# Four batches of memory attention in front of two feed-forward layers: keys, values and softmax laid out anew for batches 1 to 3

## The chip, the cores and the metric

One core of one Trainium2 chip. The time is device microseconds of one execution; lower is better. Engines in the rows: PE is TensorE (PEld its weight loads), DVE VectorE, ACT ScalarE, POOL GpSimd, SP the engine that issues all transfers here. DMA stands for the 16 transfer engines.

## The reference

There are 4 batches, 8 heads, 576 tokens, 64 values per head and 32 memory slots. Both feed-forward layers are 512 to 2048 to 512 over 4 x 576 = 2304 tokens.

```python
a = exp(phi - max(phi, tokens)); a = a / (sum(a, tokens) + 1e-9)
k_m = einsum('bhsm,bhsd->bhmd', a, k); v_m = einsum('bhsm,bhsd->bhmd', a, v)
scores = q @ k_m.T / 8                    # 576 x 32 per head
attn = softmax(scores)                    # over the 32 slots, 1e-9 added to the sum
x = attn @ v_m                            # heads side by side: 2304 x 512
h = x @ w_in;  x = max(0.01 * h, h) @ w_out
h = x @ w_in2; out = (h * tanh(log(1 + exp(h)))) @ w_out2
```

## The kernel before

The first layer runs over chunks of 288 tokens. Its hidden blocks come from the attention weights and from `v_m` multiplied into `w_in` (`win_t` by `vT_t`, line 793, giving `vw_t`). Line 1044 makes a hidden block `h_t` from `at_t` and `vw_t`; line 1077 accumulates the output `acc_t`. Operands are split into a high part (`hi_t`, rounded) and a low part (`lo_t`, the rest), and products of high and low parts are summed. The second layer works on 768 tokens at a time with seven products instead of eight (lines 1398 and 1551), and its results leave at lines 1586 to 1600 as blocks of 128 rows by 256 columns, from `x_t` and `ob_t`, into `out`.

The attention of batches 1 to 3 is done in between, for each of two groups of four heads:

- `kv_tasks`: loads `phi`, `k`, `v` with 96 rows that hold six tokens each. VectorE folds the maxima over the six (line 521), TensorE transposes them (535), VectorE reduces and makes a diagonal matrix (541, 549), TensorE spreads it over the rows (555), VectorE subtracts (562), ScalarE takes exp, VectorE folds the sums (521), TensorE sums over the rows (590) and makes the key and value memories (579, 24 small matmuls per group). `kv_norm` scales them and TensorE transposes the result (626).
- `score_tasks`: loads the queries; TensorE transposes them, three blocks at a time (673), VectorE or ScalarE copies them out. `scores` makes the scores (707) for both halves of 288 tokens. `half` does the softmax on VectorE and ScalarE, in 32 x 32 blocks that VectorE transposes (727 to 757), and splits the weights into `at_t`.

The order is not written down. Each step is a task with a price per engine and a due time, and the class `Order` simulates the engines with these prices: whenever one is free it takes the ready task that is due first, and the instructions are issued in that order. A buffer that several steps share (`Tag`, `Ring`) is handed on when its last user has ended in this simulation. A table `K` holds the due times: batch 1's attention is due 10 units before its first use (`A1`), the later ones 30 (`A2`); loads of the second layer's operands (`tscr` into `wo_t`) are due 5 units ahead (`L4T`). All transfers go through SP in one queue.

Of the kernel before, what the change touches and what calls it, by code (L numbers as in the profile page):

```python
# [10 lines left out]
F32R = mybir.dt.float32r  # L11
# [12 lines left out]
def hop(a, b):  # L24
# [10 lines left out]
    DW=280e3, DQ=1.3, DP=1.2, DS=0.78, DI=0.38, L4=0.5, L4P=1.6, L4S=0.8, L4T=5.0, MA=6, FK=-52.5, DWF=0.85, MV="......rvvrrvvrvr",  # L35
# [124 lines left out]
def kernel(  # L160
# [266 lines left out]
    def kv_first(g, p0, dp):  # L427
        sp = "s" if g else ""
        ph = tags["phi" + sp].new([P, 576] if sp else [P, HG * R * M])
        kv = tags["kv" + sp].new([P, 2304] if sp else [P, 2 * HG * R * D])  # L430
# [70 lines left out]
    def kv_tasks(b, g, p0, dp):  # L501
        if not b:
            return kv_norm(b, g, p0, dp, *kv_first(g, p0, dp))
        sp, ps_tag = "", misc
        ph = tags["phi" + sp].new([PR, HG, R, M])
        kv = tags["kv" + sp].new([P, 2, HG, R, D])
        hs = slice(g * HG, (g + 1) * HG)
        pl = p0 - 6
        l_phi = load(pl, ph.make, lambda: phi[b, hs].rearrange("h (p r) m -> p h r m", p=PR), 294912, (), [ph], (), K["DP"])

        def ld(e):
            kv.make()
            for j, x in enumerate((k, v)):
                dma(out=kv.t[:PR, j], in_=x[b, hs].rearrange("h (p r) d -> p h r d", p=PR))

        l_kv = add({"SP": K["DQ"] * mb(1179648)}, pl + 0.2, ld, (), [kv])

        def fold(buf, op):

            halves = [ph.t[:, :, r:r + R // 2].rearrange("p h r m -> p r h m") for r in (0, R // 2)]  # L520
            nc.vector.tensor_tensor(out=buf.make(), in0=halves[0], in1=halves[1], op=op)
            for r in range(NR, R // 2):
                nc.vector.tensor_tensor(out=buf.t[:, 0], in0=buf.t[:, 0], in1=buf.t[:, r], op=op)


        NR = R // 2 if b < 2 else 1

        rmax = tags["rm" + sp].new([PR, R // 2, HG, M])
        t0 = keep(add({"DVE": 0.58 if b < 2 else 1.1}, p0, lambda e: fold(rmax, ALU.max), [l_phi], [rmax], [ph]))
        mt = ps_tag.new([P, NR, PR])  # L530

        def fmt(e):
            mt.make()
            for r in range(NR):
                nc.tensor.transpose(mt.t[:, r], rmax.t[:, r].rearrange("p h m -> p (h m)"), ident[:PR, :PR])

        t1 = add({"PE": 0.1 + 0.1 * NR}, p0 + dp, fmt, [t0], [mt], [rmax])
        mx, dg = tags["mx" + sp].new([P, 1]), tags["dg" + sp].new([P, P])
        t2 = add(
            {"DVE": dve(NR * PR)}, p0 + dp,  # L540
            lambda e: nc.vector.tensor_reduce(out=mx.make(), in_=mt.t.rearrange("p r c -> p (r c)"), axis=AX.X, op=ALU.max),
            [t1], [mx], [mt],
        )

        def fdg(e):
            if e == "ACT":
                nc.scalar.activation(out=dg.make(), in_=ident, func=AF.Copy, scale=mx.t)
            else:
                nc.vector.tensor_scalar(out=dg.make(), in0=ident, scalar1=mx.t, scalar2=None, op0=ALU.mult)

        t2 = add({"ACT": 0.21, "DVE": 0.21}, p0 + dp, fdg, [t2], [dg], [mx])
        bc = ps_tag.new([PR, HG, 1, M])
        t3 = add(
            {"PE": 0.25}, p0 + 2 * dp,
            lambda e: nc.tensor.matmul(
                out=bc.make().rearrange("p h o m -> p (h o m)"), lhsT=ones, rhs=dg.t, start=True, stop=True
            ),
            [t2], [bc], [dg, mx],
        )
        t4 = add(  # L560
            {"DVE": 0.87}, p0 + 2 * dp,
            lambda e: nc.vector.tensor_tensor(
                out=ph.t, in0=ph.t, in1=bc.t.to_broadcast([PR, HG, R, M]), op=ALU.subtract
            ),
            [t3], (), [ph, bc],
        )
        t5 = [add(
            {"ACT": act(768)}, p0 + 2.5 * dp,
            lambda e: nc.scalar.activation(out=ph.t, in_=ph.t, func=AF.Exp), [t4], (), [ph],
        )]  # L570
        rs = tags["rm" + sp].new([PR, R // 2, HG, M])
        t6 = add({"DVE": 0.58 if b < 2 else 1.1}, p0 + 3 * dp, lambda e: fold(rs, ALU.add), t5, [rs], [ph])
        acc, dn = ps_tag.new([P, 2 * D]), misc.new([P, 1])

        def fkv(e):
            acc.make()
            for r in range(R):
                for h in range(HG):
                    nc.tensor.matmul(  # L579
                        out=acc.t[M * h:M * (h + 1), :].rearrange("p (j d) -> p j d", j=2),  # L580
                        lhsT=ph.t[:, h, r, :],
                        rhs=kv.t[:PR, :, h, r, :],
                        start=(r == 0),
                        stop=(r == R - 1),
                    )

        def fsums(e):
            dn.make()
            for r in range(NR):
                nc.tensor.matmul(  # L590
                    out=dn.t, lhsT=rs.t[:, r].rearrange("p h m -> p (h m)"), rhs=ones[:PR, 0:1],
                    start=(r == 0), stop=(r == NR - 1),
                )

        den, rec = tags["den" + sp].new([P, 1]), tags["rec" + sp].new([P, 1])

        t6 = add(
            {"PE": 0.2 * NR}, p0 + 3.5 * dp, fsums, [t6], [dn], [rs],
        )
        t7 = add({"PE": 1.65}, p0 + 3.8 * dp, fkv, [*t5, l_kv, t6], [acc], [ph, kv])  # L600
# [5 lines left out]
        t8 = add({"DVE": 0.25}, p0 + 4.0 * dp, fden, [t6], [den, rec], [dn])  # L606

        kv_norm(b, g, p0, dp, acc, rec, t7, t8)

    def kv_norm(b, g, p0, dp, acc, rec, t7, t8):  # L610
        sp = "s" if b < K['SB'] and g == 1 else ""
        kvn = tags["kvn" + sp].new([P, 2 * D])
# [8 lines left out]
        kt = (misc if b else acc_tag.slots[1]).new([P, P])  # L621
        kb, vb = kT_tag[g].new([P, P]), vT_tag.new([P, HG // 2, M])

        def ftr(e):
            kt.make(), kb.make(), vb.make()
            nc.tensor.transpose(kt.t, kvn.t, ident)

        t11 = add({"PE": 0.12}, p0 + 5 * dp, ftr, [t9], [kt, kb, vb], [kvn])

        ks, vs = [], []  # L630
        for j in range(2):
# [7 lines left out]
                lambda e, x=half_j, j=j: copy(e, vb.t[x], kt.t[D:2 * D].rearrange("p (a e m) -> p e a m", e=2, m=M)[:, j]),  # L639
# [5 lines left out]
    def score_tasks(b, g, pq, ps, dp):  # L645
        sp = b < K['SB'] and g == 1
        qT = (qT_s if sp else qT_tag).new([P, HG, NB1])
        parts, firsts_q = [], []
        qb = (q_s if sp else q_tag).new([P, RQ, D])
        q_g = q[b, g * HG:(g + 1) * HG]  # L650

        def ld(e):
            qb.make()
            if not b:
                dma(out=qb.t, in_=q_g.rearrange("h (p r) d -> (h p) r d", r=RQ))
                return
            for h in range(HG):
                dma(
                    out=qb.t[32 * h:32 * (h + 1)].rearrange("p (j r) d -> p j (r d)", r=2),
                    in_=q_g[h].rearrange("(j p r) d -> p j (r d)", r=2, p=32),  # L660
                )

        lq = add({"SP": (K["DQ"] if b else K["DS"]) * mb(589824)}, pq - 4 if b else PQ[g], ld, (), [qb])
        for i in range(3):
            ps_b = (misc if b else h_tag).new([P, 3, P])

            def ftr(e, ps_b=ps_b, i=i):
                ps_b.make()
                if not i:
                    qT.make()  # L670
                for j in range(3):
                    r = 2 * (3 * i + j)
                    nc.tensor.transpose(ps_b.t[:, j], qb.t[:, r:r + 2, :].rearrange("p r d -> p (r d)"), ident)  # L673

            tt = add({"PE": 0.34}, pq + 0.7 * i, ftr, [lq, *firsts_q[:1]], [ps_b] if i else [ps_b, qT], [qb])
# [15 lines left out]
        both = scores(b, g, ps[0], qT, parts, (0, 1)) if b else None
# [967 lines left out]
```

## Time and profile before

| | |
|---|---|
| median of 3 runs | 750.68 us (750.11 to 751.19) |
| the profiled execution | 751.77 us, of which its span is 750.0 |
| granted TensorE clock, mean | 0.997 of full |
| TensorE busy | 737.4 us, 98% |
| VectorE busy | 545.8 us, 73% |
| ScalarE busy | 413.1 us, 55% |
| transfers | 183.75 MB, 245 GB/s on the mean |

The span runs from the first to the last record of the core; the time of a run has some more around it. A busy share says how much of the span an engine had an instruction running, not how close to its peak. The chain goes back from the last instruction, each time to what released it; its shares say who the others waited for.

### The profile page before, as it was taken

How to read it: one execution, taken by the hardware profiler on the slowest of the kernel's cores; microseconds unless marked ns; L12 is line 12 of the kernel's file. 1: busy time of each engine (PE TensorE's matmuls, PEld its weight loads, DVE VectorE, ACT ScalarE, POOL GpSimd, SP SyncE). 2: the span in 40 equal slices, each digit the busy share in tenths (PEclk: the TensorE clock that was granted, in tenths of full speed). 3: DMA queues.
4: the chain of work that ended last, by engine and by line, in shares of the span. 5: the costliest groups of instructions: out<-in, count | busy, mean ns of one | idle time of the engine just before them, and what ended most of it. 6: DMA issues, size and time to landing. Idle time of an engine off the chain costs nothing.

```text
span 750.0 us, 15892 instructions
## 1 busy us (share of the span) xinstructions
PE 737.4 (98%) x5978; PEld 706.4 (94%) x5978; DVE 545.8 (73%) x1180; ACT 413.1 (55%) x916; POOL 0.7 (0%) x6
## 2 busy tenths in 40 slices
PE   8899999999999999999999999999999999999997
PEld 7689899988898998999999999999999999999997
DVE  6989758768676886655779798767576965665585
ACT  3867457646464656554456674644455644454443
POOL 0000000000000000000000000000000000000000
PEclk9999999999999999999999999999999999999999
DMA  9984595838869397966269988788977878987476
GB/s 345 294 286 136 176 285 169 245 122 263 239 222 320 141 300 241 308 193 215 99 247 317 351 321 293 226 265 258 322 250 245 266 246 254 290 289 224 126 214 193
DMA packets 99436, 183.75 MB, mean 245 GB/s; under 512 B 8224, under 2 KB 55328, under 8 KB 99360
## 3 DMA queue, kind: packets, MB, share of 16 engines
q1 hardware_dynamic: 99360, 182.75, 75.8%
q8 instruction: 47, 0.77, 0.4%
q14 instruction: 29, 0.24, 0.1%
HBM read 140.25 MB, written 42.47 MB: 244 GB/s over the span
## 4 chain that ended last, share of the span: by engine, by line
PE 90%; DVE 3%; DMA 3%; ACT 2%; issue 1%; SPq 0%; ACTq 0%; DVEq 0%
PE acc_t L1077 25%; PE h_t L1398 21%; PE acc_t L1551 17%; PE h_t L1044 12%; PE misc_t L1551 7%; PE misc_t L793 2%; PE acc_t L1398 2%; DMA q_t<-in_q_dram 1%; PE acc_t L485 1%; PE misc_t L579 1%; DMA rawm_t<-in_moe_w_in_dram 1%; DMA raw_t<-w2scr 1%; PE misc_t L673 1%; PE misc_t L707 1%; DVE vw_t L326 0%
## 5 line engine op out<-in xcount | busy, mean ns | idle before, releaser
L1077 PE MATMUL acc_t<-hi_t,wo_t 128*128 128x288 f32 x1024 | 163.3, 299 | 0.9 <-ACT x_t L310 0.8
L1077 PEld LDWEIGHTS acc_t<-hi_t,wo_t 128*128 128x128 f32 x1024 | 143.2, 188 | 14.0 <-issue 9.3
L1551 PE MATMUL acc_t<-wo_t,hi_t 128*128 128x256 f32 x720 | 133.7, 279 | 0.0
L1044 PE MATMUL h_t<-at_t,vw_t 128*128 128x288 f32 x768 | 124.7, 298 | 2.7 <-ACT e_t L1058 0.9
L1551 PEld LDWEIGHTS acc_t<-wo_t,hi_t 128*128 128x128 f32 x720 | 118.0, 188 | 0.2 <-DVE ob_t L312 0.2
L1044 PEld LDWEIGHTS h_t<-at_t,vw_t 128*128 128x128 f32 x768 | 109.8, 189 | 4.0 <-ACT e_t L1058 1.4
L1058 ACT ACTIVATE hi_t<-h_t 128x288 fp32r<-128x288 f32 x128 | 52.4, 410 | 110.6 <-PE acc_t L1077 89.4
L1551 PE MATMUL acc_t<-wo_t,lo_t 128*128 128x256 f32 x360 | 102.0, 283 | 0.0
L1065 DVE TENSOR_TENSOR lo_t<-e_t,hi_t 128x288 fp32r<-128x288 f32 x128 | 57.7, 454 | 54.7 <-ACT e_t L1058 28.5
L1077 PE MATMUL acc_t<-lo_t,wo_t 128*128 128x288 f32 x512 | 91.2, 300 | 0.2 <-DVE lo_t L1065 0.2
L1398 PE MATMUL h_t<-xt_t,vw_t 128*128 128x384 f32 x396 | 79.2, 336 | 0.0
L1077 PEld LDWEIGHTS acc_t<-lo_t,wo_t 128*128 128x128 f32 x512 | 74.7, 188 | 4.5 <-issue 3.6
L1520 DVE TENSOR_TENSOR lo_t<-wo_t,hi_t 128x384 fp32r<-128x384 f32 x94 | 52.0, 555 | 36.9 <-ACT hi_t L310 35.5
L1398 PE MATMUL h_t<-xt_t,wo_t 128*128 128x384 f32 x352 | 75.5, 336 | 0.0
L1551 PEld LDWEIGHTS acc_t<-wo_t,lo_t 128*128 128x128 f32 x360 | 67.6, 188 | 0.0
L1398 PEld LDWEIGHTS h_t<-xt_t,vw_t 128*128 128x128 f32 x396 | 66.7, 188 | 0.5 <-DVE wo_t L1417 0.5
L310 ACT ACTIVATE hi_t<-wo_t 128x384 fp32r<-128x384 f32 x83 | 43.4, 523 | 41.0 <-PE acc_t L1551 28.4
L1398 PEld LDWEIGHTS h_t<-xt_t,wo_t 128*128 128x128 f32 x352 | 59.5, 188 | 0.1
L1551 PE MATMUL misc_t<-wo_t,hi_t 128*128 128x256 f32 x288 | 54.1, 279 | 0.0
L1058 ACT ACTIVATE e_t<-h_t 128x288 f32<-128x288 f32 x128 | 51.8, 407 | 0.0
L1520 DVE TENSOR_TENSOR lo_t<-vw_t,hi_t 128x384 fp32r<-128x384 f32 x50 | 27.7, 555 | 25.4 <-ACT hi_t L310 25.2
L1423 ACT ACTIVATE wo_t<-wo_t 128x384 f32<-128x384 f32 x53 | 27.6, 521 | 32.9 <-DVE wo_t L1417 32.7
(219 smaller groups left out, 1079.0 us busy)
## 6 DMA issues: line engine op xcount, KB each, us to landing
wo_t<-tscr SPq DMA_DIRECT2D x168, 256.0 KB, 3.9
vw_t<-wsum SPq DMA_DIRECT2D x32, 512.0 KB, 4.7
win_t<-wscr SPq DMA_DIRECT2D x24, 512.0 KB, 5.9
raw_t<-in_moe_w_in_dram SPq DMA_DIRECT2D x19, 512.0 KB, 6.9
raw_t<-in_moe_w_out_dram SPq DMA_DIRECT2D x17, 512.0 KB, 7.7
wsum<-vw_t SPq DMA_DIRECT2D x16, 512.0 KB, 5.1
wo_t<-wsum SPq DMA_DIRECT2D x16, 512.0 KB, 4.3
kv_t<-in_k_dram SPq DMA_DIRECT2D x8, 576.0 KB, 9.8
```

The costliest lines, as they stand in the source:

```text
L310: nc.scalar.activation(out=o, in_=i, func=AF.Copy)
L485: nc.tensor.matmul(out=acc.t[rows, :].rearrange("p (j d) -> p j d", j=2), lhsT=phv()[rows, r, :], rhs=kv.t[rows, :2304].rearrange("p (j r ...
L579: nc.tensor.matmul(out=acc.t[M * h:M * (h + 1), :].rearrange("p (j d) -> p j d", j=2), lhsT=ph.t[:, h, r, :], rhs=kv.t[:PR, :, h, r, :], s ...
L793: nc.tensor.matmul(out=pss[g].t[M * (h ^ g):M * (h ^ g) + M, :], lhsT=vT[b, g][0].t[rows, h // 2, :], rhs=wbs[g].t[rows, h // 2, :], start ...
L1044: nc.tensor.matmul(out=h.t, lhsT=us[g][0].t[:, wi, j0:j0 + P], rhs=ats[g][0].t[:, ai, cols], start=(n == 0), stop=(n == 3 * NG - 1),)
L1058: nc.scalar.activation(out=o, in_=h.t, func=AF.Prelu, alpha=0.01)
L1065: lambda e: nc.vector.tensor_tensor(out=lb.make(), in0=eb.t, in1=hb.t.bitcast(F32), op=ALU.subtract),
L1077: nc.tensor.matmul(out=ac[kk].t, lhsT=wu[0].t[:, wi, kk * P:(kk + 1) * P], rhs=(hb if src == 0 else lb).t, start=(first and (wi, src) == ( ...
L1398: nc.tensor.matmul(out=h.t, lhsT=w[:, wi, c0:c0 + P], rhs=xp[b, xi].ap()[:, j], start=(first and j == 0 and k3 == 0), stop=(j == 1 and k3 ...
L1423: lambda e: nc.scalar.activation(out=t_of[x](), in_=h.t if h else t_of[x](), func=AF.Mish),
L1520: lambda e, hb=hb, lb=lb, src=src: nc.vector.tensor_tensor(out=lb.make(), in0=src(), in1=hb.t.bitcast(F32), op=ALU.subtract),
L1551: nc.tensor.matmul(out=ac[t].t, lhsT=x.t[:, t * P:(t + 1) * P], rhs=T[:, wi], start=(u == 0 and n3 == 0 and first_of), stop=(u == CH - 1 a ...
```

## The change

Batches 1 to 3 are no longer worked off group by group. `kv_rest` takes both groups at once. `phi`, `k` and `v` are loaded so that 128 rows hold two heads by 64 rows, with nine tokens each; one pass of maxima, broadcast, subtraction, exp and sums covers all eight heads. The key and value memories become 72 small matmuls per batch, each over 64 rows. Keys are transposed by VectorE, values by four matmuls. `score_rest` loads the queries with 128 rows of four heads by 32 rows, and VectorE transposes them in place in 32 x 32 blocks, so the scores are made from two 32-row contractions. One softmax covers both groups, 128 x 576 at a time. Since nine consecutive tokens lie in one row, the tokens of these batches stand in another order inside the kernel, and the output transfers put them back (`out_j`). Buffers are shared anew, and batch 0 changes only in its buffers.

```diff
...
+    RB = 9
+    def kv_rest(b, p0, dp):
+        ph = tags["phi"].new([P, HG, RB, M])
+        kv = [kvq.new([P, 2, 2, RB, D]) for _ in range(NG)]
...
+        pairs = lambda x: x[b].rearrange("(x e) (t j) d -> (e t) x j d", e=2, j=RB)
...
+        def fold(buf, op, last):
+            xs = ph.t.rearrange("p x j m -> p j x m")
+            b4 = buf.make()
+            nc.vector.tensor_tensor(out=b4, in0=xs[:, 0:4], in1=xs[:, 4:8], op=op)
+            nc.vector.tensor_tensor(out=b4[:, 0:2], in0=b4[:, 0:2], in1=b4[:, 2:4], op=op)
+            nc.vector.tensor_tensor(out=b4[:, 0], in0=b4[:, 0], in1=b4[:, 1], op=op)
+            last(b4[:, 0], xs[:, 8])
...
+            for j in range(RB):
+                for x in range(HG):
+                    for y in range(2):
+                        g, h = x // 2, 2 * (x % 2) + y
+                        rows, o = slice(D * y, D * y + D), M * (h ^ g)
+                        nc.tensor.matmul(
+                            out=accs_[g].t[o:o + M, :].rearrange("p (j d) -> p j d", j=2),
+                            lhsT=ph.t[rows, x, j, :],
+                            rhs=kv[g].t[rows, :, x % 2, j, :],
...
+            for g in range(NG):
+                for y in range(2):
+                    nc.tensor.matmul(out=vt.t[D * y:D * (y + 1), g], lhsT=kvn.t[:, g, 1], rhs=ident, start=True, stop=True)
...
+    def score_rest(b, pq, ps, dp):
...
+                {"DVE": dve(1152) + 0.1}, pq + 0.7 * g, lambda e, flat=flat: nc.vector.transpose(out=flat(), in_=flat()), [ld0], (), [qs[g]],
...
+                for y in range(2):
+                    for h in range(HG):
+                        for g in range(NG):
+                            rows, o = slice(M * h, M * (h + 1)), M * (h ^ g)
+                            nc.tensor.matmul(
+                                out=pss[g].t[o:o + M, :].rearrange("p (r i) -> p r i", i=M),
+                                lhsT=kb.t[rows, g, y, :],
+                                rhs=q_of[g]()[rows, RB * hf:RB * (hf + 1), y, :],
...
-        for g in range(NG):
-            p = base[b] - d + st * g
-            kv_tasks(b, g, p, 0.08 * d / 2)
-            score_tasks(b, g, p + 0.1 * d, (p + 0.3 * d, p + 0.4 * d), 0.03 * d)
+        p = base[b] - d
+        kv_rest(b, p, 0.08 * d / 2)
+        score_rest(b, p + 0.1 * d, (p + 0.3 * d, p + 0.3 * d + st), 0.03 * d)
...
+    out_j = [out[x // 2 * S:(x // 2 + 1) * S].rearrange("(i u j) f -> u j i f", u=2, j=RB)[x % 2] for x in range(2 * B)]
...
-                            dma(out=out_b[hf][p0:p0 + n, k2 * 256:(k2 + 1) * 256], in_=ob.ap()[o:o + n, :])
+                            cs = slice(k2 * 256, (k2 + 1) * 256)
+                            if hf < 2:
+                                dma(out=out_b[hf][p0:p0 + n, cs], in_=ob.ap()[o:o + n, :])
+                            else:
+                                dma(out=out_j[hf][p0 // M:(p0 + n) // M, :, cs], in_=ob.ap()[o:o + n, :])
```

Two places show how the instructions move. The first is TensorE in batch 1, from the broadcast of the maxima to the key and value memories, before; the names are those of the section on the kernel, `misc_t` being a PSUM buffer.

```order
L555 MATMUL misc_t<-dg_t,ones 96x128
L1077 MATMUL acc_t<-hi_t,wo_t 128x288 x8
L1077 MATMUL acc_t<-lo_t,wo_t 128x288 x4
L1077 MATMUL acc_t<-hi_t,wo_t 128x288 x8
L1077 MATMUL acc_t<-lo_t,wo_t 128x288 x4
L793 MATMUL misc_t<-win_t,vT_t 32x512 x8
L1077 MATMUL acc_t<-hi_t,wo_t 128x288 x8
L1077 MATMUL acc_t<-lo_t,wo_t 128x288 x4
L1077 MATMUL acc_t<-hi_t,wo_t 128x288 x8
L590 MATMUL misc_t<-ones,rm_t 128x1 x3
L1044 MATMUL h_t<-at_t,vw_t 128x288 x6
L579 MATMUL misc_t<-kv_t,phi_t 32x128 x24
```

The same stretch after the change (L1226 is line 1077 of before, L943 is 793; L557 spreads the maxima, L597 sums, L620 makes the memories).

```order
L557 MATMUL misc_t<-rm_t,ones 64x128 x2
L1226 MATMUL acc_t<-hi_t,wo_t 128x288 x8
L1226 MATMUL acc_t<-lo_t,wo_t 128x288 x4
L1226 MATMUL acc_t<-hi_t,wo_t 128x288 x8
L1226 MATMUL acc_t<-lo_t,wo_t 128x288 x4
L1226 MATMUL acc_t<-hi_t,wo_t 128x288 x8
L1226 MATMUL acc_t<-lo_t,wo_t 128x288 x4
L1226 MATMUL acc_t<-hi_t,wo_t 128x288 x8
L597 MATMUL misc_t<-ones,rm_t 128x1 x2
L1226 MATMUL acc_t<-lo_t,wo_t 128x288 x4
L943 MATMUL misc_t<-win_t,vTb_t 32x512 x8
L620 MATMUL misc_t<-kvq_t,phi_t 32x128 x72
```

One pass for both groups stands there. The step 793 has moved from before the sums to behind them, all accumulating groups at hand stand between broadcast and sums, and the memory products are one block of 72 instead of 24. The second place is the end of SP's queue, before: the last output transfers.

```order
L279 DMA wo_t<-tscr_5050 128x512
L279 DMA out_dram<-x_t 128x256 x2
L279 DMA out_dram<-ob_t 128x256
L279 DMA out_dram<-ob_t 64x256 x2
L279 DMA out_dram<-x_t 128x256
L279 DMA out_dram<-ob_t 128x256
L279 DMA out_dram<-ob_t 64x256 x2
L279 DMA out_dram<-x_t 128x256
```

And after the change.

```order
L279 DMA wo_t<-tscr_4896 128x512
L279 DMA out_dram<-x_t 4x32x256 x2
L279 DMA out_dram<-ob_t 4x32x256
L279 DMA out_dram<-ob_t 2x32x256 x2
L279 DMA out_dram<-x_t 4x32x256
L279 DMA out_dram<-ob_t 4x32x256
L279 DMA out_dram<-ob_t 2x32x256 x2
L279 DMA out_dram<-x_t 4x32x256
```

The same transfers stand there in the same order, and those of 128, 96 and 64 rows have become four, three and two blocks of 32 rows.

## Rows read from the trace of the kernel before

**Rows 1.** The page, busy time and share of the span by engine; chain by engine.

```profile
...
PE 737.4 (98%) x5978; PEld 706.4 (94%) x5978; DVE 545.8 (73%) x1180; ACT 413.1 (55%) x916; POOL 0.7 (0%) x6
...
PE 90%; DVE 3%; DMA 3%; ACT 2%; issue 1%; SPq 0%; ACTq 0%; DVEq 0%
```

**Rows 2.** Waits of TensorE over the span: total us, times, longest.

```profile
...
PE acc_t L485 <- DMA kv_t<-in_v_dram: 1.4, 1, 1.4
```

**Rows 3.** Chain at the end: start us, us, what.

```profile
...
741.38 3.56 PE acc_t L1551 x30
...
745.74 0.35 DVE x_t L1586
```

**Rows 4.** Transfers from 732.6 to 750 us: GB/s in 40 slices; issues, KB, us to landing.

```profile
...
GB/s 245 146 184 304 252 115 68 146 348 339 351 339 221 148 179 132 320 353 351 297 318 341 278 137 217 134 153 247 0 0 0 202 99 151 94 177 181 0 0 0
...
wo_t<-tscr SPq DMA_DIRECT2D x5, 256.0 KB, 4.4
out_dram<-x_t SPq DMA_DIRECT2D x6, 128.0 KB, 3.7
out_dram<-ob_t SPq DMA_DIRECT2D x2, 128.0 KB, 2.5
out_dram<-ob_t SPq DMA_DIRECT2D x4, 64.0 KB, 2.1
out_dram<-x_t SPq DMA_DIRECT2D x2, 96.0 KB, 4.0
```

**Rows 5.** Chain from 60 to 85 us (batch 1, second group): start us, us, what.

```profile
...
66.25 0.33 PE misc_t L673 x3
...
67.36 0.25 PE misc_t L535 x3
...
69.56 0.22 PE misc_t L555 x2
...
73.76 0.56 PE misc_t L590 x6
...
74.57 1.45 PE misc_t L579 x48
...
76.87 0.11 PE misc_t L626
...
78.04 0.79 PE misc_t L707 x16
...
81.14 1.02 PE misc_t L793 x16
```

**Rows 6.** TensorE by line and shape, whole span: busy us, mean ns.

```profile
...
L673 PE MATMUL misc_t<-ident,q_t 128*128 128x128 f32 x54 | 9.0, 280 | 0.0
```

**Rows 7.** Chain from 150 to 162 us (batch 2).

```profile
...
151.64 0.12 PE misc_t L590 x2
```

**Rows 8.** Stretch, its length, then busy us: PE, PEld, DVE, ACT, POOL.

```profile
...
41.00:54.00 13.00, 12.68 (x102) 11.33 (x101) 9.31 (x19) 7.92 (x19) 0.00 (x0) 1.00 0.96 300
54.00:75.00 21.00, 20.55 (x221) 19.25 (x223) 19.39 (x49) 16.01 (x40) 0.00 (x0) 1.00 0.42 122
```

**Rows 9.** VectorE by line and shape, whole span.

```profile
...
L757 DVE STREAM_TRANSPOSE T_t<-T_t 128x288 f32<-128x288 f32 x16 | 7.5, 468 | 0.0
...
L521 DVE TENSOR_TENSOR rm_t<-phi_t 96x384 f32<-96x384 f32 x12 | 6.5, 544 | 1.4 <-ACT phi_t L569 1.3
...
L562 DVE TENSOR_TENSOR phi_t<-phi_t,misc_t 96x768 f32<-96x768 f32 x6 | 5.6, 940 | 1.3 <-PE misc_t L555 1.2
...
L523 DVE TENSOR_TENSOR rm_t<-rm_t 96x128 f32<-96x128 f32 x16 | 4.6, 288 | 0.6
```

**Rows 10.** The last output transfer, 748.05 to 748.65 us, 40 slices.

```profile
...
DMA  0011915957939909919939559249127020000000
...
DMA packets 145, 0.13 MB, mean 219 GB/s; under 512 B 17, under 2 KB 145, under 8 KB 145
...
q1 hardware_dynamic: 145, 0.13, 62.6%
```

More of the change, by code (lines that the diff above doesn't have):

```diff
@@ L499, in kv_first @@
         return acc, rec, t4, t3
[L501 to L507, printed above, removed]
-        pl = p0 - 6
[L509 to L538, printed above, removed]
@@ L545, in fdg @@
         def fdg(e):
[L546 to L559, printed above, removed]
+            dg.make()
@@ new lines, in fdg, with fbc @@
+            for x in range(2):
+                if e == "ACT":
+                    nc.scalar.activation(out=dg.t[:, x], in_=ident, func=AF.Copy, scale=mx.t[:, x:x + 1])
+                else:
+                    nc.vector.tensor_scalar(out=dg.t[:, x], in0=ident, scalar1=mx.t[:, x:x + 1], scalar2=None, op0=ALU.mult)
+        t2 = add({"ACT": 0.7, "DVE": 0.4}, p0 + dp, fdg, [t2], [dg], [mx])
+        bc = misc.new([P, HG, 1, M])
+        def fbc(e):
+            bc.make()
+            for x in range(2):
+                nc.tensor.matmul(
+                    out=bc.t[D * x:D * (x + 1)].rearrange("p h o m -> p (h o m)"), lhsT=ones[:, :D], rhs=dg.t[:, x],
+                    start=True, stop=True,
+                )
@@ L569, in kv_tasks @@
             lambda e: nc.scalar.activation(out=ph.t, in_=ph.t, func=AF.Exp), [t4], (), [ph],
[L570 to L585, printed above, removed]
+        )
@@ new lines, in kv_rest, with last_sum @@
+        rs = tags["rm"].new([P, 4, HG, M])
+        def last_sum(x, y):
+            lo_, hi_ = slice(0, D), slice(D, 2 * D)
+            rsx = rs.t.rearrange("p l x m -> p (l x m)")[:, P:P + 320]
+            nc.vector.memset(rsx, 0.0)
+            halves = lambda z, c: z[c].rearrange("p (g a) m -> p g a m", g=NG)
+            nc.vector.tensor_tensor(
+                out=rsx[lo_].rearrange("p (g c) -> p g c", g=NG)[:, :, :P].rearrange("p g (a r) -> p g a r", a=2)[:, :, :, :M],
+                in0=halves(x, lo_), in1=halves(y, lo_), op=ALU.add,
+            )
+            for g in range(NG):
+                nc.vector.tensor_tensor(
+                    out=rsx[hi_, g * P:(g + 1) * P].rearrange("p (a r m) -> p a r m", a=2, m=M)[:, :, 1 - g],
+                    in0=halves(x, hi_)[:, g], in1=halves(y, hi_)[:, g], op=ALU.add,
+                )
@@ L587, in fsums @@
+        t6 = add({"DVE": 1.9}, p0 + 3 * dp, lambda e: fold(rs, ALU.add, last_sum), [t5], [rs], [ph])
+        dn = misc.new([P, NG])
         def fsums(e):
             dn.make()
-            for r in range(NR):
+            for g in range(NG):
                 nc.tensor.matmul(
-                    out=dn.t, lhsT=rs.t[:, r].rearrange("p h m -> p (h m)"), rhs=ones[:PR, 0:1],
-                    start=(r == 0), stop=(r == NR - 1),
-                )
-        den, rec = tags["den" + sp].new([P, 1]), tags["rec" + sp].new([P, 1])
@@ L597, in kv_tasks @@
[L597 to L600, printed above, removed]
+                    out=dn.t[:, g:g + 1], lhsT=rs.t.rearrange("p l x m -> p (l x m)")[:, (g + 1) * P:(g + 2) * P],
+                    rhs=ones[:, 0:1], start=True, stop=True, skip_group_check=True,
+                )
+        t6 = add({"PE": 0.2}, p0 + 3.5 * dp, fsums, [t6], [dn], [rs])
+        den, rec = tags["den"].new([P, NG]), tags["rec"].new([P, NG])
@@ L604, in fden, with fkv @@
             nc.vector.reciprocal(out=rec.make(), in_=den.t)
-        t8 = add({"DVE": 0.25}, p0 + 4.0 * dp, fden, [t6], [den, rec], [dn])
-        kv_norm(b, g, p0, dp, acc, rec, t7, t8)
+        t8 = add({"DVE": 0.34}, p0 + 3.6 * dp, fden, [t6], [den, rec], [dn])
+        accs_ = [misc.new([P, 2 * D]) for _ in range(NG)]
+        def fkv(e):
+            for x in accs_:
+                x.make()
+            for j in range(RB):
[7 more added lines that the diff above has]
+                            rhs=kv[g].t[rows, :, x % 2, j, :],
+                            start=(j == 0),
+                            stop=(j == RB - 1),
+                        )
@@ new lines, in kv_rest, with fn @@
+        t7 = add({"PE": 2.2}, p0 + 3.8 * dp, fkv, [t5, *l_kv, t6], accs_, [ph, *kv])
+        kvn = tags["rm"].new([P, NG, 2, D])
+        tn = []
+        for g in range(NG):
+            def fn(e, g=g):
+                if not g:
+                    kvn.make()
+                o = kvn.t[:, g].rearrange("p j d -> p (j d)")
+                if e == "ACT":
+                    nc.scalar.activation(out=o, in_=accs_[g].t, func=AF.Copy, scale=rec.t[:, g:g + 1])
+                else:
+                    nc.vector.tensor_scalar(out=o, in0=accs_[g].t, scalar1=rec.t[:, g:g + 1], scalar2=None, op0=ALU.mult)
+            tn.append(add(
+                {"ACT": act(P, True), "DVE": dve(P)}, p0 + 4.3 * dp, fn, [t7, t8, *tn], [] if g else [kvn], [accs_[g], rec] + ([kvn] if g else []),
+            ))
@@ new lines, in kv_rest, with fk @@
+        kb, vb, vt = kT_tag[0].new([P, NG, 2, M]), vTb_tag.new([P, NG, HG, M]), misc.new([P, NG, P])
+        tk = []
+        for g in range(NG):
+            def fk(e, g=g):
+                if not g:
+                    nc.vector.transpose(out=kb.make()[:, 0].rearrange("p e m -> p (e m)"), in_=kvn.t[:, 0, 0])
+                    return
+                for h in range(HG):
+                    i, o = slice(M * (h ^ g), M * (h ^ g) + M), slice(M * h, M * h + M)
+                    nc.vector.transpose(out=kb.t[o, g].rearrange("p e m -> p (e m)"), in_=kvn.t[i, g, 0])
+            tk.append(keep(add({"DVE": 0.85 if g else 0.22}, p0 + 5 * dp, fk, [tn[g], *tk], [] if g else [kb], [kvn, kb] if g else [kvn])))
@@ new lines, in ftr @@
+        def ftr(e):
+            vt.make(), vb.make()
+            for g in range(NG):
+                for y in range(2):
+                    nc.tensor.matmul(out=vt.t[D * y:D * (y + 1), g], lhsT=kvn.t[:, g, 1], rhs=ident, start=True, stop=True)
+        t11 = add({"PE": 0.45}, p0 + 5 * dp, ftr, tn, [vt, vb], [kvn])
+        tv = keep(add(
+            {"ACT": act(2 * P, True), "DVE": dve(2 * P)}, p0 + 5.2 * dp,
+            lambda e: copy(e, vb.t.rearrange("p g h m -> p g (h m)"), vt.t), [t11], (), [vt, vb],
+        ))
@@ L653, in ld @@
             qb.make()
[L654 to L663, printed above, removed]
+            dma(out=qb_v(), in_=q_g.rearrange("h (p r) d -> (h p) r d", r=RQ))
+        lq = add({"SP": K["DS"] * mb(589824)}, PQ[g], ld, (), [qb])
         for i in range(3):
-            ps_b = (misc if b else h_tag).new([P, 3, P])
+            ps_b = h_tag.new([P, 3, P])
             def ftr(e, ps_b=ps_b, i=i):
                 ps_b.make()
-                if not i:
+                if sp and not i:
                     qT.make()
@@ L709, in fsc @@
                         lhsT=kT[b, g][0].t[rows, M * h:M * (h + 1)],
-                        rhs=qT.t[rows, h, :],
+                        rhs=qT_v()[rows, h, :],
                         start=True,
@@ L718, in scores, with half @@
         return {hf: (t, *p) for hf, p in zip(hfs, bufs)}
-    def half(b, g, hf, ps, dp, qT, parts, a, ab, both):
+    def half(b, g, hf, ps, dp, qT, qT_v, parts, a, ab):
         nb = NB32 // 2
         sp = b < K['SB'] and g == 1
-        ts, T, ps_b = (both or scores(b, g, ps, qT, parts, (hf,)))[hf]
+        ts, T, ps_b = scores(b, g, ps, qT, qT_v, parts, (hf,))[hf]
         flat = lambda t: t.rearrange("p n m -> p (n m)")
@@ L754, in half @@
         )
-        T2 = (T2_s if sp else T2_tag).new([P, NB1])
-        t6 = add(
-            {"DVE": dve(NB1)}, ps + 3.5 * dp, lambda e: nc.vector.transpose(out=T2.make(), in_=flat(T.t)), [t5], [T2], [T]
-        )
+        t6 = add({"DVE": dve(NB1)}, ps + 3.5 * dp, lambda e: nc.vector.transpose(out=flat(T.t), in_=flat(T.t)), [t5], (), [T])
         cols = slice(hf * NB1, (hf + 1) * NB1)
@@ L902 @@
                 wo_unit(m)
-    kv_again = tags["kv"].new([P, 3, 1024])
-    opened = add({"SP": 0.0}, K["W2"], lambda e: kv_again.make(), (), [kv_again])
+    kv_again = [kvq.new([P, 2, 1024]) for _ in range(2)]
+    opened = [add({"SP": 0.0}, K["W2"], lambda e, x=x: x.make(), (), [x]) for x in kv_again]
     class View:
@@ L911, in __init__ @@
             self.j, self.res, self.bufs = j, Res(1), []
-            self.res.after = [opened]
+            self.res.after = [opened[j // 2]]
         def new(self, shape, dtype=F32):
```

185 lines of the change are left out of this document (142 added, 43 removed).

## The prediction

> **What bounds the kernel now.** I read the page first, then TensorE's waits, then the chain of the stretch that the change rewrites, then the queue's last 18 us. TensorE is busy 98% of the span and holds 90% of the chain; VectorE is at 73% [rows 1]. Its longest named wait is 1.4 us, in the first microseconds [rows 2]. So whatever the change takes from or adds to TensorE's instructions of batches 1 to 3 arrives almost one for one at TensorE's end. That is not yet the end of the program: the chain ends with matmuls to 744.94, three VectorE adds, and then output transfers [rows 3], whose bytes run to about 748.7 [rows 4] (the last slice that moved anything is the 37th of 0.435 us each). Two sums are needed: TensorE's work, and the transfers behind it.
>
> **TensorE's work, batch by batch.** One profiled record is one pass; an fp32 matmul shows as two.
>
> - Query transposes: six groups of three per batch, 0.33 us each [rows 5], gone because VectorE does it in place. 3 x 6 x 0.33 = 5.9 us off. The 54 records that go [rows 6] agree.
> - Maxima: batch 1 transposes 2 x 0.25 [rows 5], the later ones 2 x 0.11 (as the single transposes of that view); now one, 0.11. Broadcast: 2 x 0.22 becomes about 0.25. Together 1.2 off over three batches.
> - Sums: 2 x 0.56 in batch 1, 2 x 0.12 later [rows 5, 7]; now two instructions, 0.12. 1.2 off.
> - Key/value products: 48 records in 1.45 us per group [rows 5]. They sit on four column tiles, so 12 rounds; with 0.15 for filling and draining, (1.45 - 0.15) / 12 = 0.108 per round. After: 144 records for both groups on eight tiles (two row halves by four column quarters), 18 rounds, 18 x 0.108 + 0.15 = 2.1 instead of 2.90. 2.4 off.
> - Value transposes: 2 x 0.11 becomes four 64-column matmuls, eight records on two column tiles, 4 x 0.108 = 0.43. 0.6 on.
> - Scores: 16 records in 0.79 per group, 1.58 a batch [rows 5]. After, the contraction is cut into two 32-row parts: 2 halves of 32 records on eight tiles, four rounds each. A round of 288 columns, from the 512-column ones (16 records on eight tiles in 1.02 us, two rounds, 0.43 each [rows 5]): 0.43 x 288/512 = 0.245. 2 x (4 x 0.245 + 0.15) = 2.26. 2.1 on.
>
> Sum: -5.9 - 1.2 - 1.2 - 2.4 + 0.6 + 2.1 = -8.0 us, 1.1% of TensorE.
>
> This rests on row halves running side by side where they write one bank of PSUM, as the new key/value matmuls do. The row that bears on it is the 512-column one: eight tiles, two of each bank's four quarters fed by either row half. One by one, 16 records at 0.43 would take 6.8 us; they take 1.02. I therefore count eight at a time. If only four ran at once, the products would cost 36 x 0.108 + 0.15 = 4.0 and each half's scores 8 x 0.245 + 0.15 = 2.1, together 3.9 more a batch, 11.8 in all.
>
> [...]
>
> **New waits on TensorE.** Batch 1's chain is the short one. Before, VectorE is busy 9.31 of the 13 us from 41 to 54 us [rows 8], so 3.7 are free. VectorE's price, 1.03 ns an element from 384 to 768 elements and about 0.15 to start [rows 9]: a 1152-element transpose 1.37 (from the 0.468 of 288), two of them 2.7; the maxima 0.68 + 0.42 + 2 x 0.29 = 1.7 against 0.54; the subtraction 1.34 against 0.94; the sums about 2.3 against 0.54. That is 6.1 us more, 2.4 beyond what is free. Behind it on VectorE stand the low halves (`lo_t`) that TensorE's accumulating matmuls consume; in the new order all of these that are at hand stand between broadcast and sums, with step 793 behind them instead of between. ScalarE is busy 7.92 of the 13 and can take some copies, so I take half, 1.2 us; 0 and 3 bound it. Later batches have 30 units of lead instead of 10, and cost nothing here. Queries leave the queue in 128-row pieces instead of four pieces of 32 rows; that may give up to 2 us back before 40 us, taken as 0 since no row names TensorE as waiting for them.
>
> **The output transfers.** The source rows of an output block are no longer consecutive tokens. Its destination becomes 4 (or 3, or 2) blocks of 32 rows that lie 18 tokens apart, where it was one run of 128, 96 or 64 rows, two tokens apart. Before, such a transfer is spread over all engines: the last one's 128 packets of 1 KB were 62.6% of 16 engines for 0.6 us, 6.0 us of packet time, 47 ns a packet, done in 31 slices of 0.015 us, so about 13 engines were at work at a time [rows 10]. No row of before has a transfer whose slowest dimension is 4. Lower bound: still spread, 0. Upper bound: shared out by that dimension, so that the first engine carries a whole 32-row block, 32 packets instead of 8 (also for 3 and 2 blocks). 32 x 47 ns is 1.5 us a transfer instead of 0.38.
>
> From 732.6 us on there are 14 such transfers: 6 + 2 of 128 KB, 4 of 64, 2 of 96 [rows 4]. They, and five 256 KB loads at about 350 GB/s (0.75 us each [rows 4], 3.7 together), then queue on the first engine from 734.3: 14 x 1.5 + 3.7 = 24.7, to 759, where it was 748.7: 10.3 later. With twelve engines idle a packet may take less; at 43 ns it is 8.5, and I take that. The loads behind them land about 2 us later than their 4.4 median; loads are issued five units (about 9 us) ahead, so this is covered, there and near 640 us, where the same outputs pass.
>
> I choose the upper end, not the lower. The rows can't tell them apart: every transfer of before has an outer dimension that is a multiple of 16, so one that is cut at its outer dimension and one that is cut anywhere would look alike there. That an outer dimension of 4 offers four equal shares at once and no sixteen is what decides me.
>
> [...]
>
> **Sum.** -8.0 + 1.2 + 8.5 = +1.7 us on the profiled 751.77, 753.5. The median of the runs lies 1.1 below the profiled one, so 752.4.
>
> **Rivals.**
> 1. The outputs stay spread: TensorE's gain shows at the end. -8.0 + 1.2 = -6.8: 744 (743 to 747). For it: all transfers seen so far are spread, and the bytes are the same. Against it: only shapes with 32, 64, 96 or 128 as the outer size have been seen. It decides at once: no transfer needs to be late, and the end is 3 to 4 us behind TensorE's, as before.
> 2. Only four small tiles at a time: +11.8 on the forecast, 764, or 756 with spread outputs. The 512-column row speaks against it.
> 3. VectorE holds up batch 1, and its in-place transposes and sums also the later batches: some 4 us more, 756, or 748 with spread outputs. For it: VectorE is busy 19.39 of the 21 us from 54 to 75. Against it: the second group's whole pass, which made it so, is folded into the first.
>
> **Chances and range.** Forecast 0.55, rival 1 0.28, rival 2 0.05, rival 3 0.12. About 0.2% (1.5 us) is what can be told from no change here. Within the forecast (749.5 to 755.5, from 43 to 47 ns a packet and 0 to 3 us of stall, and from a backlog that is partly drained) slower has 0.31, same 0.20, faster 0.04. Rival 1 gives faster 0.26, same 0.02; rival 2 slower 0.05; rival 3 slower 0.08, same 0.02, faster 0.02. Sum: faster 0.32, same 0.24, slower 0.44. The range that leaves out 2 in 10 reaches into rival 1: 744 to 755.5.
>
> **What would show it.** The key/value products: about 2.1 us per batch, scores 1.1 per half; 4 and 2.1 would be rival 2. TensorE's last matmul some 7 us earlier, near 738. The output transfers: landing 5 us and more after their issue at the end against a median near 3 before, with the share of the 16 engines low while the queue is full; the last bytes 12 or more after TensorE's end. If they land in 2 to 4 us, the forecast is wrong and rival 1 holds. Between 41 and 60 us a wait of TensorE for VectorE's low halves of 1 to 2 us; more there, or near 150 and 235 us, is rival 3.

## The result, and the profile after

| | before | after |
|---|---|---|
| median | 750.39 us (749.86 to 751.19) | 761.11 us (759.31 to 761.22) |
| ratio to before | | 1.0136 [1.0118, 1.0154] |
| span of the profiled execution | 750.0 us | 759.3 us |

The change makes the kernel 1.4% slower. The forecast said slower, with 752.4 and at most 755.5. The page of the changed kernel, first busy time by engine, then the granted TensorE clock, then the chain [rows 1]:

```profile
...
PE 733.2 (97%) x6167; PEld 700.9 (92%) x6167; DVE 545.0 (72%) x1137; ACT 404.0 (53%) x883; POOL 0.7 (0%) x6
...
PEclk9999999999999999999999999999999999999997
...
PE 92%; DVE 2%; DMA 2%; ACT 1%; issue 1%; SPq 0%; DVEq 0%; ACTq 0%
```

TensorE's busy time fell by 4.2 us while the span grew by 9.3. The chain says where, with TensorE's end and a load in front of it (start us, us, what; [rows 3]):

```profile
...
737.81 6.88 DMA wo_t<-tscr
...
744.83 0.61 PE acc_t L1701 x3
```

On the chain TensorE ends at 745.44, where it ended at 744.94, so nothing of the forecast gain is left there. From the end of the chain's last VectorE add to the end of the span it is now 12.7 us (746.6 to 759.3), where it was 3.9 (746.1 to 750.0). These two differences, 0.5 and 8.8, are the 9.3. The transfers at the end, 732 to 760 us: share of the 16 engines in tenths, then GB/s, each in 40 slices, then issues [rows 4]:

```profile
...
DMA  6468788667762222222222222221122111111000
GB/s 221 83 110 307 181 258 177 221 214 217 230 262 102 97 85 98 88 82 98 95 98 72 73 97 69 94 85 50 50 70 95 70 48 48 48 47 41 1 0 0
...
wo_t<-tscr SPq DMA_DIRECT2D x5, 256.0 KB
out_dram<-x_t SPq DMA_DIRECT2D x6, 128.0 KB
```

The rate stands at 97, then 70, then 48 GB/s, with 0.26 of the 16 engines busy from 744.9 to 750 us and 0.14 from 754 to 757: from these an estimate of 4, 3 and 2 engines at about 24 GB/s each. Before, the transfers of this stretch moved at up to 353 [rows 4]. The last load before TensorE's end took 6.88 us against a median of 4.4 before.

The new small matmuls, in the chain of batch 2 [rows 5, 7] (start us, us, what):

```profile
...
144.05 2.18 PE misc_t L620 x144
...
148.83 0.59 PE misc_t L663 x8
...
155.23 1.02 PE misc_t L943 x16
...
159.37 1.13 PE misc_t L709 x32
...
162.29 1.13 PE misc_t L709 x32
```

Key/value products take 2.18 us and scores 1.13 per half, as worked out. But TensorE now has these waits (us in total, times, longest) [rows 2]:

```profile
...
PE misc_t L620 <- DVE vw_t L326: 2.5, 2, 2.4
...
PE acc_t L1226 <- DVE lo_t L1214: 1.4, 2, 1.1
...
PE acc_t L1701 <- DMA wo_t<-tscr: 1.3, 3, 0.7
```

The wait for `vw_t` is that of the key/value products in batch 1. Of the 1.4 us for `lo_t`, 1.1 lie before 41 us, so between 41 and 60, where the forecast had put 1 to 2 us, it is 0.3. In batch 1 there are these stretches (length, busy us of PE, PEld, DVE, ACT, POOL, then the granted clock, the share of the transfer engines and GB/s):

```profile
...
58.00:61.00 3.00, 0.65 (x16) 0.15 (x8) 2.90 (x6) 3.00 (x7) 0.00 (x0) 1.00 0.91 318
61.00:64.00 3.00, 2.82 (x111) 2.82 (x115) 2.96 (x7) 1.91 (x4) 0.00 (x0) 0.51 0.57 183
64.00:67.00 3.00, 2.35 (x49) 1.81 (x34) 1.04 (x3) 0.78 (x3) 0.00 (x0) 0.92 0.02 5
```

Between 58 and 61 us TensorE is busy for 0.65 of 3 us, with VectorE full. Then its clock is granted at about half for three microseconds. The key/value products that were to take 2.1 us begin to wait at 58.2 and end only at 65.8. Their records (start us, us, engine and line; in brackets the idle time before and what ended it), and VectorE's step that ended the first wait:

```profile
...
60.58 0.42 PE L620 MATMUL misc_t<-kvq_t,phi_t 64*32 64x128 f32 x8 [2.35 <-DVE vw_t L326]
61.18 3.56 PE L620 MATMUL misc_t<-kvq_t,phi_t 64*32 64x128 f32 x126 [0.18 <-DVE vw_t L326]
65.39 0.43 PE L620 MATMUL misc_t<-kvq_t,phi_t 64*32 64x128 f32 x10 [0.65 <-issue]
...
59.85 1.28 DVE L326 TENSOR_TENSOR vw_t<-misc_t,vw_t 128x512 fp32r<-128x512 f32 x2
```

### The profile page after: what moved, and what is told of

It reads as the page before. It is cut to its first block, busy times and chain, and to the rows that moved or that the text cites. A ratio compares the mean times of both kernels' runs of the same rounds, so it can differ in the third digit from the quotient of the medians.

```text
span 759.3 us, 16148 instructions
## 1 busy us (share of the span) xinstructions
PE 733.2 (97%) x6167; PEld 700.9 (92%) x6167; DVE 545.0 (72%) x1137; ACT 404.0 (53%) x883; POOL 0.7 (0%) x6
## 4 chain that ended last, share of the span: by engine, by line
PE 92%; DVE 2%; DMA 2%; ACT 1%; issue 1%; SPq 0%; DVEq 0%; ACTq 0%
PE acc_t L1226 27%; PE h_t L1547 21%; PE acc_t L1701 16%; PE h_t L1193 13%; PE misc_t L1701 6%; PE acc_t L1547 2%; PE misc_t L943 2%; PE misc_t L620 1%; DMA kvq_t<-in_q_dram 1%; PE acc_t L484 1%; DMA wo_t<-tscr 1%; PE misc_t L709 1%; PE acc_t L1024 1%; PE h_t L833 0%; DVE raws_t L387 0%
## 5 line engine op out<-in xcount | busy, mean ns | idle before, releaser
L1226 PE MATMUL acc_t<-hi_t,wo_t 128*128 128x288 f32 x1024 | 161.5, 298 | 0.4 <-ACT at_t L310 0.3
L1226 PEld LDWEIGHTS acc_t<-hi_t,wo_t 128*128 128x128 f32 x1024 | 143.7, 188 | 10.3 <-issue 4.7
L1226 PE MATMUL acc_t<-lo_t,wo_t 128*128 128x288 f32 x512 | 90.6, 299 | 1.4 <-DVE lo_t L1214 1.4
L1226 PEld LDWEIGHTS acc_t<-lo_t,wo_t 128*128 128x128 f32 x512 | 74.6, 188 | 8.7 <-issue 6.2
```

The costliest lines, as they stand in the source:

```text
L1226: nc.tensor.matmul(out=ac[kk].t, lhsT=wu[0].t[:, wi, kk * P:(kk + 1) * P], rhs=(hb if src == 0 else lb).t, start=(first and (wi, src) == ( ...
```

## Experiments

Theory 1: the output transfers are carried by as few engines as their outer dimension has entries, and that is the 8.8 us. Theory 2: the stall in batch 1 comes from VectorE's queue and eats most of TensorE's gain.

**The kernel before with the new output addresses.**

```diff
...
+    out_j = [out[x // 2 * S:(x // 2 + 1) * S].rearrange("(i u j) f -> u j i f", u=2, j=9)[x % 2] for x in range(2 * B)]
...
-                            dma(out=out_b[hf][p0:p0 + n, k2 * 256:(k2 + 1) * 256], in_=ob.ap()[o:o + n, :])
+                            cs = slice(k2 * 256, (k2 + 1) * 256)
+                            if hf < 2:
+                                dma(out=out_b[hf][p0:p0 + n, cs], in_=ob.ap()[o:o + n, :])
+                            else:
+                                dma(out=out_j[hf][p0 // M:(p0 + n) // M, :, cs], in_=ob.ap()[o:o + n, :])
```

> The kernel before, with one edit: the output transfers of batches 1 to 3 use the destination addresses of the changed kernel (4, 3 or 2 blocks of 32 rows), so the rows of the output stand in another order; the bytes, their number and everything else stay. Theory 1 (a transfer is shared out by its outer dimension, so 4, 3 or 2 transfer engines carry it): TensorE's end stays near 745 to 748 (loads of wo_t queue behind outputs, up to 2 us), the last bytes come about 13 us after it instead of 3, the rate falls to about 100, 70 and 50 GB/s at the end, and the time is 760 to 763. Rival (the tail of the changed kernel comes from its other timing, not from these transfers): 750 to 752.

761.1 us, ratio 1.012 [1.0097, 1.0144]. GB/s from 735 to 760 us in 40 slices:

```profile
...
GB/s 272 174 256 275 174 272 305 108 95 98 100 97 97 95 97 97 84 79 69 95 95 98 92 51 49 66 80 98 54 46 49 49 48 33 3 0 0 0 0 0
```

The same steps, and the span ends 12.7 us after the last VectorE add, as in the changed kernel. TensorE ends at 743.82, a little below what was expected. This edit alone costs the kernel before nearly what the whole change costs. Loads for TensorE are late too, though the named wait is only:

```profile
...
PE acc_t L1552 <- DMA wo_t<-tscr: 0.6, 2, 0.4
```

**The same addresses in pieces of 32 rows.**

```diff
...
-                                dma(out=out_j[hf][p0 // M:(p0 + n) // M, :, cs], in_=ob.ap()[o:o + n, :])
+                                for jj in range(n // M):
+                                    dma(out=out_j[hf][p0 // M + jj, :, cs], in_=ob.ap()[o + M * jj:o + M * (jj + 1), :])
```

> The changed kernel, with each output transfer of batches 1 to 3 cut into transfers of 32 rows, to the same addresses. Theory 1 (sharing by the outer dimension): 32 rows are shared by 16 engines, the loads are no longer late and TensorE ends near 743.5; but there are 46 small transfers instead of 14 from 732 us on, at about 0.35 to 0.45 us of issue each, so the queue itself may be late by some us: 749 to 755. Rival (the scattered destination, rows 18 tokens apart, is what is slow, whoever carries it): the rate at the end stays at 50 to 100 GB/s and the time at 759 to 762.

760.38 us, ratio 1.0113 [1.0091, 1.0136]: slower than expected, and the time of the rival. The rate doesn't settle it; the issues and landings do. SP from 738 us on (start us, us, then the operation), and KB and median us to landing:

```profile
...
738.67 6.27 SPq L279 DMA_DIRECT2D out_dram<-x_t  x12
745.03 3.61 SPq L279 DMA_DIRECT2D out_dram<-ob_t  x8
...
754.31 1.76 SPq L279 DMA_DIRECT2D out_dram<-x_t  x4
```

```profile
...
out_dram<-x_t SPq DMA_DIRECT2D x30, 32.0 KB, 1.6
out_dram<-ob_t SPq DMA_DIRECT2D x16, 32.0 KB, 1.6
```

Each piece lands 1.6 us after its issue, below the medians of before (2.1 to 4.0 [rows 4]), into the same scattered rows: the addresses are not slow. But 36 of them at 0.44 to 0.52 us keep SP issuing until 756, 12 us after TensorE. The price moved from the engines to the queue. I had expected the queue to be late by some us, not by all of it. TensorE ends at 743.61, as expected, and from 600 us to there the profile names no wait of TensorE.

**The old token order, by a strided read.**

```diff
...
-                                out=pss[g].t[o:o + M, :].rearrange("p (r i) -> p r i", i=M),
+                                out=pss[g].t[o:o + M, :].rearrange("p (i r) -> p i r", i=M),
...
-                                rhs=q_of[g]()[rows, RB * hf:RB * (hf + 1), y, :],
+                                rhs=q_of[g]()[rows, hf:RQ:2, y, :].rearrange("p r i -> p i r"),
...
```

The scores are still written side by side; only the reading is strided. The outputs are then again those of `out_b`.

> The changed kernel, but the score matmuls read the transposed queries with a stride, so that the tokens come out in the old order and the output transfers are those of the kernel before. Theory 1: the tail is as before (last bytes 3 to 4 us after TensorE), no late loads; of the 9.3 us of span that the change cost 8.8 come back at the end and 2.0 in TensorE's last 10 us: 749.5 to 751.5. That it isn't faster than before would be the stall in batch 1 (theory 2). Price of the stride: a round of 288 columns stays at 0.24 us, 1.13 us for 32 records; a rival has the strided read slower, up to twice, 1.1 us more per half, 7 in all. If the gain of 8.0 us on TensorE that was forecast is there in full: 743 to 744.

757.58 us, ratio 1.007 [1.0046, 1.0094]. The span ends 3.9 us after the last VectorE add, so the tail is gone, but the scores show the rival's price (chain, batch 2):

```profile
...
162.15 2.57 PE misc_t L709 x23
...
166.51 2.56 PE misc_t L709 x24
```

2.57 us instead of 1.13. The stride of 512 bytes more than doubles them, which is 8.6 us in six halves and more than the rival's 7.

**The old token order, by the load.**

```diff
...
-                dma(out=flat(), in_=q[b, g * HG:(g + 1) * HG].rearrange("h (p r) d -> (h p) (r d)", r=RQ))
+                for h in range(HG):
+                    dma(
+                        out=flat()[32 * h:32 * (h + 1)].rearrange("p (j x) -> p j x", j=RB),
+                        in_=q[b, g * HG + h].rearrange("(j p r) d -> p j (r d)", r=2, p=32),
+                    )
...
-                                rhs=q_of[g]()[rows, RB * hf:RB * (hf + 1), y, :],
+                                rhs=q_of[g]()[rows, hf:RQ:2, y, :],
...
```

The outputs go by `out_b` again.

> The changed kernel, but the queries of batches 1 to 3 are loaded as in the kernel before (four transfers per group, runs of 512 bytes), so that after the in-place transposes two tokens of a pair lie side by side; the scores read every second block, contiguous inside a block of 32, and the output transfers are those of the kernel before. It differs from the strided run only in that. Theory 1 (the tail alone, and the stride cost TensorE the rest there): scores 1.13 us per half again, TensorE ends near 743.5 to 745, the last bytes 3 to 4 us later: 748.5 to 751. Rival (something else than the tail and the stride holds TensorE up): 753 or more.

752.15 us, ratio 1.0029 [1.0013, 1.0045], a little above what was expected.

```profile
...
158.02 1.13 PE misc_t L713 x32
...
162.54 1.13 PE misc_t L713 x32
```

The scores cost 1.13 again, the tail is 3.8 us, and 9 us of the change's loss are gone with the output transfers. TensorE ends at 745.37, though, no earlier than in the changed kernel, and has waits at the key/value products for which the profile names no releaser ("issue"):

```profile
...
PE misc_t L620 <- issue: 5.7, 4, 2.1
```

Two of them, 1.6 and 0.2 us in batch 1, end 0.1 us after VectorE's two low halves of `vw_t`, as in the changed kernel. The other two, 1.8 us in batch 1 and 2.1 in batch 3, stand inside the block of products; they are taken up below.

**Batch 1 without its query transposes.**

```diff
...
-                {"DVE": dve(1152) + 0.1}, pq + 0.7 * g, lambda e, flat=flat: nc.vector.transpose(out=flat(), in_=flat()), [ld0], (), [qs[g]],
+                {"DVE": dve(1152) + 0.1}, pq + 0.7 * g, lambda e, flat=flat: None if b == 1 else nc.vector.transpose(out=flat(), in_=flat()), [ld0], (), [qs[g]],
```

> The changed kernel in the same planned order, but VectorE leaves out the two 1152-element query transposes of batch 1 (2.7 us at 46.4 and 48.2 us), so batch 1's scores are those of untransposed queries. Theory 2 (TensorE's stall before and in the key/value products of batch 1, 58 to 65.4 us, comes from VectorE's queue, which the transposes lengthen): the wait of 2.35 us for vw_t goes to 0 to 0.5, the granted clock no longer falls to half there, and the time falls by 3 to 5 us, to 756 to 758. Rival (the weights for that step come late by the transfers that the new loads stand in front of): the wait stays above 2 us and the time within 1 us of 761.

759.46 us, ratio 1.0106 [1.0076, 1.0135]; the interval overlaps that of the changed kernel. VectorE's busy time from 41 to 54 us (third of the busy times) fell from 12.08, in the changed kernel, to 8.41, here:

```profile
...
41.00:54.00 13.00, 13.00 (x98) 12.49 (x98) 12.08 (x24) 8.53 (x21) 0.00 (x0) 1.00 0.53 199
```

```profile
...
41.00:54.00 13.00, 13.00 (x91) 12.67 (x90) 8.41 (x19) 7.33 (x18) 0.00 (x0) 0.90 0.49 198
```

and the wait did not move:

```profile
...
PE misc_t L620 <- DVE vw_t L326: 2.5, 2, 2.4
```

So theory 2 in that form falls: it is not the amount of VectorE's work in front. The wait names `vw_t`, but the key/value products read only `kvq_t` and `phi_t`. What they need of the `vw_t` step is its buffers: `misc_t` has two, the new products take both at once, and the step in front of them holds both until VectorE has made its low halves, behind the weight conversions in its queue. In the changed kernel the first eight records start 0.1 us after the first low half and the next as the second ends (59.85 to 61.13 us). That is theory 2b.

**Batch 1 due earlier.**

```diff
...
-    LAG1=2, WIN=8, OB=2, RS=4, FILL=36, A1=10, S1=2.8,
+    LAG1=2, WIN=8, OB=2, RS=4, FILL=36, A1=14, S1=2.8,
```

> The changed kernel with one number changed: batch 1's attention is due 14 units before its first use instead of 10. In the planned order the key/value products then stand before the vw_t step instead of behind it. Theory 2b (the stall comes from these products needing both PSUM buffers of misc_t at once, behind a vw_t step whose eviction is queued on VectorE): the wait of 2.4 us and the half clock behind it go, TensorE ends 2 to 5 us earlier, and the time falls from 761 to 756 to 759. Rival (batch 1 is short of VectorE whatever the order, as the run without the transposes suggests it isn't, or short of transfers): TensorE's waits between 41 and 75 us only move, and the time stays within 1 us of 761.

756.01 us, ratio 1.0088 [1.007, 1.0106]. The order puts the products ahead of the `vw_t` step, and the stretches of batch 1 read

```profile
...
58.00:61.00 3.00, 2.29 (x25) 1.06 (x23) 2.93 (x6) 1.74 (x4) 0.00 (x0) 1.00 0.10 18
61.00:64.00 3.00, 2.87 (x40) 1.83 (x41) 2.96 (x7) 2.07 (x6) 0.00 (x0) 1.00 0.83 332
64.00:67.00 3.00, 3.00 (x47) 2.19 (x46) 3.00 (x8) 2.11 (x5) 0.00 (x0) 1.00 0.00 0
```

with the clock at full throughout. From 41 to 75 us one wait is left:

```profile
...
PE misc_t L709 <- DVE vw_t L326: 0.8, 1, 0.8
```

TensorE ends 5.2 us earlier (740.25), the tail stays at 12.6. VectorE is as full as before, so the wait of 2.4 us was the order and the buffers. The number moves other steps too; a third buffer alone was not tried.

The half clock is another matter. In the strided run, with the order of the changed kernel and the clock at 1.00 from 58 to 64 us, the block reads as follows; the last line is the queue that the profile calls `instruction`, from 62 to 64 us (packets, MB, share of the 16 engines):

```profile
...
59.87 2.01 PE L620 MATMUL misc_t<-kvq_t,phi_t 64*32 64x128 f32 x126 [0.17 <-DVE vw_t L326]
64.74 0.43 PE L620 MATMUL misc_t<-kvq_t,phi_t 64*32 64x128 f32 x10 [2.86 <-issue]
...
q8 instruction: 1, 0.02, 2.8%
```

The 126 records took 2.01 us instead of 3.56, and the last ten waited 2.86 us instead of 0.65. From its first record to its last the block took 5.9 us there and 5.2 in the changed kernel, so the half clock isn't shown to have cost anything inside it. I take the wait in front of the last records for one for TensorE's own instructions; that is inferred, not shown. In the six runs that have it, it ends 1.0 to 1.6 us after a transfer of 16 KB in that queue has landed (in the changed kernel at 65.39, the landing at 63.78). Counted over all TensorE records of the trace, it stands at record 1473 (batch 1), 4545 or 4801 (batch 3), and the last two lie 12 and 13 times 256 behind the first. The changed kernel has 48 such transfers (below) for 12334 records of matmuls and weight loads, which gives an estimate of 257 to a transfer, while the block has 288 in some 2 us.

```profile
...
q8 instruction: 48, 0.79, 0.4%
```

With 14 the block ends at record 1412, ahead of 1473, so that run took away both waits at once; no run separates them.

**Both.** The old order by the load, and 14.

> Both edits together: the queries loaded in the old token order with the old output transfers, and batch 1 due 14 units ahead. Theory 1 and 2b: 745 to 748, below the kernel before (750.7) by what TensorE saves; if the stall only moves, 749 to 751.

746.75 us (745.95 to 747.03), ratio 0.9958 [0.9946, 0.9971], faster than both kernels, and 0.4% faster than the kernel before.

```profile
span 744.1 us, 16176 instructions
...
PE 731.0 (98%) x6167; PEld 698.3 (94%) x6167; DVE 545.5 (73%) x1138; ACT 403.7 (54%) x882; POOL 0.7 (0%) x6
...
PEclk9999999999999999999999999999999999999999
```

TensorE's end is at 739.13 and the span 5 us after it.

**Batches 2 and 3 due earlier as well** (`A2` 34 instead of 30):

> As the run before, with batches 2 and 3 due 34 units ahead instead of 30. If nothing waits for them at 30, as the waits of TensorE say, the time is the same within 1 us; if their VectorE work collides with the running layer, 1 to 3 us less.

747.1 us, ratio 0.9964 [0.9952, 0.9976]: the same, so nothing waited for them.

## Why the prediction was wrong

The sign was right, the size was not: +10.7 us, forecast +1.7. Point by point:

- **The output transfers: right.** The forecast had 8.5 us for the tail, chosen against rival 1; measured 8.8 behind TensorE, the same in the kernel before with only that edit. That a transfer of 4 blocks goes to four engines was an estimate that no run of before shows; the changed kernel has 97, 70 and 48 GB/s for 4, 3 and 2 blocks. About 24 GB/s per engine is a packet of 1 KB every 43 ns. That pick, against the 47 of [rows 10], had no row behind it, so that it came out is luck: from 754 to 757.5 us the 172 packets of the changed kernel take 13.7% of 16 engines, 45 ns each.
- **"This is covered" was wrong.** The loads behind the outputs were to be 2 us late and hidden. The last one took 6.88 us, and 1.3 us of waits carry its name. From one start to the next the second layer's matmuls of lines 1701 and 1551 take 180.5 us after and 178.5 before, 178.5 in the versions without the blocks and with pieces of 32 rows. Some 2 us.
- **The stall in batch 1 was the step that failed.** I took 1.2 us, bounded by 3, from VectorE's free time, as a wait for the low halves `lo_t`; that wait came to 0.3 us. Two others came instead: 2.4 us for a block that needs both buffers of a pair behind a step that holds them, and a second wait inside that block. Together they cost about 4.5 us net: 5.2 at TensorE's end between the changed kernel and the run with 14, of which 0.7 is later loads. The first is shown. That the second is TensorE's own instructions is argued, and how it and the half clock share the rest stays open. I had found the order in which `vw_t` stands ahead without asking whose buffers it holds.
- **TensorE's work: right in kind, too large.** The run with both edits, without blocks and without those two waits, against the kernel before is -5.8 us by TensorE's ends in the two profiled executions (739.13 and 744.94), and only -3.5 by the medians of the runs (746.75 and 750.21), instead of -8.0. Products and scores came as forecast. The 0.15 us for filling and draining stands in no row by itself; it was an estimate, and 1.45 us for 12 rounds of 128 columns and 1.02 for two of 512 [rows 5] give 0.16, if a round grows with its columns. Two small terms were too low: four value transposes take 0.59 us a batch, not 0.43; a pair of sums takes about 0.4, not 0.12. That is 1.3 us in all, and the rest isn't accounted for. The rows (busy us, mean ns):

```profile
...
L663 PE MATMUL misc_t<-ident,rm_t 128*64 128x128 f32 x24 | 2.0, 285 | 0.0
...
L597 PE MATMUL misc_t<-ones,rm_t 128*128 128x1 f32 x12 | 1.5, 229 | 0.0
```

- **Rival 2** (four tiles at a time) is out: 2.18 and 1.13 us fit eight at a time (forecast 2.1 and 1.1) and not four (4.0 and 2.1), two row halves into one bank, and four row quarters for the scores. Here the row tiles that run together always write different quarters of a bank.
- **Rival 3** (VectorE holds up batch 1 and the later ones) came near in size, some 4 us more, and would have given 756 with the tail. Its mechanism isn't borne out: with less VectorE work the wait stayed, and from 75 to 300 us the profile of the changed kernel names no wait of TensorE.

Sum by what was measured: -5.8 + 4.5 + 2 + 8.8 = 9.5 against 9.3 of span. The terms are differences between single executions, and most share an end, so that they add up proves little: the 19 runs of the kernel before in the last comparison lie between 748.31 and 753.82 us. The tail is clear of that; differences of 2 us and less between TensorE's ends are not.

## What to carry to other kernels

When a layout is changed to save work on the busiest engine, follow the data to the last transfer: what counted here was the outer dimension of the destination, 97 GB/s with 4 blocks and 48 with 2, while cutting it into many small ones moved the price into the issuing queue, 0.44 to 0.52 us each. Merging two passes into one doubles what the pass holds at once; look for who holds the second buffer, and let the merged step be due earlier. The long dense block of 144 records also had waits inside it, 0.65 us in the changed kernel and 2.86 in the strided run: look at what the trace calls "issue" before you put the time down to the clock.

## What was not expected of the hardware

After the wait of 2.4 us the granted clock stood at 0.51 from 61 to 64 us, after 1.00 from 58 to 61, while the run with the old load, busy 2.34 of 4 us from 54 to 58 us and 1.16 of 3 from 61 to 64, kept 1.00. In the strided run the block behind the same wait ran at full clock and took no less time: its last records waited 2.86 us, until 1.5 us after a transfer in the `instruction` queue had landed. A moving operand read with a stride of 512 bytes took 2.57 us for a half's scores where blocks of 32 contiguous values took 1.13. Transfers of 32 KB were issued at one per 0.44 to 0.52 us and landed in 1.6 us.
